# The opening of a fused attention and expert kernel: embeddings scaled earlier, the second group loaded in two parts, zeros by another engine

## The chip, the cores and the metric

The kernel runs on one core of a Trainium2 chip. The metric is the device time of one execution in microseconds (us); several executions are timed and the median is taken. A profile records one execution.

The engines are named as in the profile: PE (matrix multiply) with PEld (its weight loads), DVE (vector), ACT (scalar, activation), POOL (general) and SP (issues transfers only). Each works through its own instructions in program order and waits for others by semaphores. POOL and SP issue transfers between device memory and on-chip memory.

## The reference

Attention over 8 batches and 8 heads, with 576 positions and 64 columns, followed by a layer of eight experts of which each token takes one:

```python
cum    = cumsum(max(s, 0))
scores = q @ k.T / sqrt(64)
scores = where(causal, -1e9, scores + min(-(cum[:, None] - cum[None, :]), 0))
attn   = softmax(scores)                      # per head
x      = (attn @ v) heads side by side        # 4608 tokens x 512
en     = emb / (norm(emb) + 1e-6)             # 8 experts x 512
logits = (x / norm(x)) @ en.T / tau
e      = argmax(logits);  gate = softmax(logits)[e]
out    = gate * (max(x @ w1[e], 0) @ w2[e])
```

## The kernel before

All 64 heads are worked one after another, then the experts. Heads are numbered n and lie in groups g of four; a group's transposed queries and keys are loaded together (`load(g)`) into one of three buffers `qkbs[g % 3]`: 64 rows of Q (2560 columns, the region `0:QW`) beside 64 rows of K (2304 columns, `QW:`). Rows 64 to 127 hold ones under Q, and under K zeros with a few rows for the cumulative sums and the row maxima. `kzeros(i)` writes the zeros, `qones(i)` the ones, `krow(i)` a constant row 96 into the K side.

Products are in split precision: `qkbs` holds high parts, and `QCs`, `KCs` hold for each pair of heads a copy of the high part in one half of the rows and the low part in the other. For group 0 the high parts are made on chip (`round0`, ACT), copied (`hcopy`, ACT) and subtracted (`qlow` on DVE, `klow` on POOL). For later groups ACT writes the negated high part (`neg`) and a transfer on POOL's queue adds the original onto it (`addl`).

A head n takes these steps: `s1` to `s4` compute the scores once for the maxima of the rows (PE), `sr` and the reductions in `s3`, `s4` take them (DVE); after every second head `mrow1`, `mrow2` transpose the maxima and `sends()` sends them back into row 96 of `qkbs`. Then `ta_`, `tb_`, `tbl` compute the scores again, transposed, with the maxima and the cumulative sums inside the product; `expa`, `expb1` take the exponential on ACT; `pl_` makes the low part of the probabilities (POOL, `psub`, line 242); `pv` multiplies with V (PE). The score phase runs several heads ahead: with head n goes the score phase of head m = n + 3 in the opening.

V is not used as it is: `emm(n)` multiplies V with a matrix `en4` (PE), which holds the identity and, beside it, the scaled expert embeddings, so that attention gives the router's logits as well. `vsq` sums the squares of V (ACT), `vscale` and `vcp` scale the result. The embeddings `em` are scaled once, in these steps: `ra` (ACT: the sum of squares, its square root through logarithm and exponential), `rb` (DVE and POOL: the temperature and `en4`'s constant part), `rc` (DVE: a reciprocal), `rd` (POOL: three tiny operations that refine the root), `rc` again, `re` (POOL: `r7`, lines 567 and 568, which scale `em`), and last `r7s[0]()`, that is `r8` (PE: four transposes, line 573; DVE: two copies into `en4`).

The order on each engine is the order of the calls, written by hand (a manual schedule). `begin()` is the opening: the set-up, `rows(0)` to `rows(2)` (the score phase of the first three heads, with `heat` matmuls between, which compute nothing that is used), then a loop over n = 0, 1, 2 with the first three heads' second phase, then the part with m = 6 which starts `pv(0)`. Then the loop `step(n)` runs from n = 3. In the opening, `load(1)` brings group 1 in one transfer, and the lines around the embeddings are:

```python
        ra()
        kzeros(2)
...
            if n == 0:
                rc()
                rd()          # behind s4(m), ahead of expb1(0)
...
            if n == 1:
                sends()
                rc()
                re()          # ahead of pl_(1) on POOL
...
            if n == 1:
                addl(1, False)
                r7s[0]()
                emm(0)
```

Of the kernel before, what the change touches and what calls it, by code (L numbers as in the profile page):

```python
# [8 lines left out]
F32 = mybir.dt.float32  # L9
# [15 lines left out]
QW = HG * SP  # L25
# [81 lines left out]
def main(ctx, tc, qkh, qkc, vtin, s_in, emb, tau, w1h, w2h, out, shared, nb):  # L107
# [50 lines left out]
    nc.vector.memset(one, 1.0)  # L158

    def kzeros(i):  # L160
        nc.scalar.copy(qkbs[i][64:128, QW:], zero[64:128].to_broadcast([64, KW]))

    def round0(i):
        nc.scalar.copy(qkbs[0][0:64, 2 * SP * i:2 * SP * i + 2 * SP], qrs[i])
# [2 lines left out]
    def qones(i):  # L167
        nc.gpsimd.memset(qkbs[i][64:128, 0:QW].bitcast(F32), 1.0)

    def krow(i):  # L170
        nc.gpsimd.dma_start(qkbs[i][96:97, QW:], qkc)
    kzeros(0)
    nc.scalar.copy(qkbs[0][64:128, 0:QW], one[64:128].to_broadcast([64, QW]))
    nc.gpsimd.memset(mS, 0.0)
    nc.gpsimd.affine_select(out=mS[:, 448:576], in_=mS[:, 448:576], pattern=[[-1, 128]],
# [1 line left out]
    nc.vector.memset(tiny, 1.0e-30)  # L177
    nc.vector.memset(tri0, 0.0)
    nc.vector.memset(tri, 1.0)
    nc.vector.memset(qkbs[1][64:128, QW:].bitcast(F32), 0.0)  # L180
    nc.vector.tensor_scalar(st, st, 0.0, 8.0, op0=ALU.max, op1=ALU.mult)
    nc.vector.tensor_tensor_scan(cum, st, st, 0.0, op0=ALU.add, op1=ALU.bypass)
    nc.vector.tensor_copy(chl[:, 0, :], cum)
# [57 lines left out]
    def psub(out, a, b_):  # L241
        nc.gpsimd.tensor_tensor(out, a, b_, op=ALU.subtract)  # L242

    def load(g):
        if g >= NGg:
            return
        qkb = qkbs[g % 3]
        if g > 0:
            nc.gpsimd.dma_start(qkb[0:64, :], qkh[g], **(dict(max_dma_last_dim=4864) if g < 3 else {}))
        G[g] = dict(QB=qkb[:, 0:QW].rearrange("p (h s) -> p h s", h=HG), KB=qkb[:, QW:].rearrange("p (h s) -> p h s", h=HG))  # L250

    def loadc(g):
# [11 lines left out]
    def vsq(b, ps):  # L264
        if not 0 <= b < nb:
            return
        if ps[0] == 0:
            VB[b]["sq"] = p2.tile([128, 4], F32, name="sq")
        for p in ps:
            nc.scalar.activation(vjunk, vTs[b % 2][:, p], AF.Square, accum_out=VB[b]["sq"][:, p:p + 1])  # L270
# [40 lines left out]
    def hcopy(g, k, i):  # L311
        if 0 <= g < NGg:
            h = pair(i)
            o, t = (KCs[g % 2][64:128, h], G[g]["KB"][0:64, h]) if k else (QCs[g % 2][0:64, h], G[g]["QB"][0:64, h, 64:SP])
            nc.scalar.copy(o, t.bitcast(F32))

    def neg(g, k, i):
        if 0 <= g < NGg:
            h = pair(i)
            o, t = (KCs[g % 2][0:64, h], G[g]["KB"][0:64, h]) if k else (QCs[g % 2][64:128, h], G[g]["QB"][0:64, h, 64:SP])  # L320
            nc.scalar.activation(o, t.bitcast(F32), AF.Copy, scale=-1.0)
# [9 lines left out]
    def klow(i):  # L331
        h = pair(i)
        psub(KCs[0][0:64, h], krs[i].rearrange("p (h s) -> p h s", h=2), G[0]["KB"][0:64, h].bitcast(F32))

    def qlow(i):
        h = pair(i)
        nc.vector.tensor_sub(QCs[0][64:128, h], qrs[i].rearrange("p (h s) -> p h s", h=2)[:, :, 64:SP], G[0]["QB"][0:64, h, 64:SP].bitcast(F32))
# [54 lines left out]
    def s3(n):  # L392
        if n >= NH:
            return
        p1 = ps_s.tile([128, 512], F32, tag="s", name="s3")
        smax_mm(n, 4, p1[:, 0:288], 0, 288)
        nc.vector.tensor_reduce(MP["4", n // 2][:, n % 2:n % 2 + 1], p1[:, 0:288], AX.X, ALU.max)  # L397
# [77 lines left out]
    def tbl(n):  # L475
        tb = HD[n]["tb"]
        for f in (hh_, hl_):
            f(n, tb[:, 512:704], 3, 384, 576)
        hh_(n, tb[:, 0:64], 4, 512, 576)
        mask(tb[:, 0:192], trim[:, 0:192])  # L480
        hl_(n, tb[:, 0:64], 4, 512, 576, True)
        mask(tb[:, 512:896].rearrange("p (a b) -> p a b", b=192)[:, :, 0:128], trib.unsqueeze(1).to_broadcast([128, 2, 128]), stop=True)
# [5 lines left out]
    def expb1(n):  # L488
        nc.scalar.activation(HD[n]["P32"][:, 576:1600], HD[n]["tb"], AF.Exp, scale=0.125)  # L489
# [435 lines left out]
    def rows(m):  # L925
        s1(m)
        heat(1)
        sr(m, 3)
        s2(m)
        heat(1)  # L930
        sr(m, 2)
        sr(m, 1)
        s3(m)
        heat(2)
        s4(m)
        heat(2)
        mrow1(m)

    def sends():
        rq.popleft()()  # L940
        aslot()

    def begin():
        make_identity(nc, ident)
        masks()
        load(0)
        loadc(1)
        nc.gpsimd.dma_start(krs[1], qkh[0][:, QW + 2 * S:])
        load(1)
        krow(0)  # L950
        krow(1)
        ra, rb, rc, rd, re = rsetup()
        rb()
        hset(0)
        for i in range(2):
            round0(i)
            hcopy(0, False, i)
            hcopy(0, True, i)
        qlow(0)
        klow(0)  # L960
        klow(1)
        ra()
        kzeros(2)
        rows(0)
        rows(1)
        sends()
        qlow(1)
        for p in range(2):
            loadt(0, pair(p))
        nc.sync.dma_start(cumd.rearrange("x r s -> r x s").bitcast(F32), chl.bitcast(F32))  # L970
        rows(2)
        hset(1)
        qones(1)
        setup2()
        neg(1, True, 0)
        for n in range(3):
            m = n + 3
            ta_(n, m)
            sr(m, 3)
            expa(n)  # L980
            if n == 0:
                neg(1, False, 0)
                neg(1, True, 1)
            if n == 1:
                sends()
                rc()
                re()
                neg(1, False, 1)
                vsq(0, range(4))
            if n == 2:  # L990
                vscale(0)
                fslot()
                while tasks:
                    slot()
                vcp(0, False)
                vcp(1, False)
            s2(m)
            tb_(n)
            sr(m, 2)
            sr(m, 1)  # L1000
            if n == 2:
                vcp(0, True)
                vcp(1, True)
            s3(m)
            tbl(n)
            s4(m)
            if n == 0:
                rc()
                rd()
            expb1(n)  # L1010
            if n == 1:
                hcopy(1, True, 0)
            mrow1(m)
            if n < 2:
                pl_(n, 0, 576, "p")
                if n == 0:
                    load(2)
                pl_(n, 576, 1600, "p")
            if n == 2:
                qones(2)  # L1020
                krow(2)
            if n == 0:
                addl(1, True)
            if n == 1:
                addl(1, False)
                r7s[0]()
                emm(0)
                emm(1, om)
        m = 6
        s1(m)  # L1030
        sr(m, 3)
        sends()
        s2(m)
        pv(0, [0, 1, 2])
        sr(m, 2)
        sr(m, 1)
        s3(m)
        emm(2)
        pv(0, [3, 4])
        s4(m)  # L1040
        hcopy(1, True, 1)
        vcp(2, False)
        hcopy(1, False, 0)
        vcp(2, True)
        hcopy(1, False, 1)
        loadc(2)
        loadt(1, pair(0))
        pl_(2, 0, 576, "p")
# [399 lines left out]
```

## Time and profile before

| | us |
|---|---|
| median of 3 runs | 780.52 (780.29 to 781.52) |
| the profiled execution | 781.86 |
| its span, first to last instruction | 780.1 |
| PE busy in it | 759.8 (97%) |
| DVE, ACT, POOL busy | 523.5, 570.9, 383.5 |
| start of the loop `step(n)` on PE | 45.9 |

A row of a timeline gives the start of an instruction from the span's start, its duration, engine and line, output and input, and in brackets how long the engine had been idle and what ended that. A row of a table of stretches gives for each engine the busy time in that stretch, and the TensorE clock that was granted (1.00 is full).

### The profile page before, as it was taken

The numbers are of one execution on the slowest core, as the hardware profiler recorded it, in microseconds if no ns is written. First come the engines' busy times: TensorE is split into PE (matmuls) and PEld (weight loads), VectorE is DVE, ScalarE is ACT, GpSimd is POOL, SyncE is SP. The second block draws the span as 40 slices with busy tenths as digits, with TensorE's granted clock in tenths as the row PEclk, the third lists the DMA queues.
The fourth block names the chain that finished last, engine by engine and source line by source line (L and its number), as shares of the span: only waits on it lengthen the run. The fifth ranks groups of instructions, "written<-read, shape, count | busy, mean of one in ns | idle before, by whom it ended". The sixth has DMA issues, their size and how long they took to land. (4 is left out here: it accounts for less than half of the span.)

```text
span 780.1 us, 19394 instructions
## 1 busy us (share of the span) xinstructions
PE 759.8 (97%) x7276; PEld 569.3 (73%) x7276; DVE 523.5 (67%) x1773; ACT 570.9 (73%) x1012; POOL 383.5 (49%) x370
## 2 busy tenths in 40 slices
PE   7699999999999999999999999999999999999997
PEld 3689999999999999996567557466475574664753
DVE  8477888888888888868675656655665466556621
ACT  9688999999999999988675767837658468376410
POOL 9766798989888798785412131221221211312001
PEclk9799999999999999999999999999999999999999
DMA  7775879797979797764634765753754558645001
GB/s 157 174 170 110 178 173 212 167 216 171 213 165 218 160 218 174 194 218 158 217 94 135 172 178 163 170 186 95 208 179 99 168 166 154 194 96 141 12 15 55
DMA packets 75936, 123.79 MB, mean 159 GB/s; under 512 B 38774, under 2 KB 39178, under 8 KB 74980
## 3 DMA queue, kind: packets, MB, share of 16 engines
q0 software_dynamic: 19568, 69.68, 38.2%
q1 hardware_dynamic: 56272, 52.84, 24.7%
q8 instruction: 58, 0.95, 0.5%
q14 instruction: 38, 0.31, 0.1%
HBM read 93.99 MB, written 21.49 MB: 148 GB/s over the span
## 5 line engine op out<-in xcount | busy, mean ns | idle before, releaser
L242 POOL TENSOR_TENSOR PL<-P 128x576 f16<-128x576 f32 (+2 forms) x128 | 205.0, 1705 | 24.7 <-ACT P L486 17.1
L852 PEld LDWEIGHTS <-wt 128*128 128x128 f16 x1536 | 149.7, 98 | 59.5 <-DVE wt L840 0.5
L852 PE MATMUL h<-xH,wt 128*128 128x320 f16 (+2 forms) x1024 | 186.7, 299 | 0.0
L882 POOL DMA_INDIRECT out<-Kx,xj x39 | 40.8, 1046 | 167.3 <-DVE Kx L881 105.9
L720 POOL DMA_INDIRECT Qx<-xs,idx x40 | 42.3, 1058 | 141.0 <-ACT hp L861 84.1
L514 PE MATMUL om<-vh,P 128*128 128x73 f16 x960 | 106.9, 199 | 0.9 <-DVE xt L539 0.6
L515 PE MATMUL om<-vl,P 128*128 128x72 f16 x960 | 106.2, 196 | 0.0
L852 PE MATMUL h<-xL,wt 128*128 128x320 f16 (+1 forms) x480 | 106.1, 297 | 0.0
L516 PE MATMUL om<-vh,PL 128*128 128x73 f16 x960 | 106.0, 197 | 0.0
L352 PE MATMUL s<-qkb 96*128 96x288 f32 (+4 forms) x272 | 97.5, 372 | 3.9 <-DVE M L397 1.7
L515 PEld LDWEIGHTS <-P 128*128 128x128 bf16 x960 | 94.6, 99 | 1.4 <-issue 0.9
L876 PE MATMUL pxs<-wt,hp 128*128 128x512 f16 x351 | 94.8, 379 | 0.0
L514 PEld LDWEIGHTS <-P 128*128 128x128 bf16 x960 | 93.7, 98 | 0.7 <-DVE xt L539 0.4
L516 PEld LDWEIGHTS <-PL 128*128 128x128 f16 x960 | 93.9, 98 | 0.0
L876 PE MATMUL pxs<-wt,hq 128*128 128x512 f16 x351 | 88.8, 379 | 0.1
L360 DVE CUSTOM_DVE_ANT_0 junk<-s,mS 128x448 bf16<-128x448 f32 (+3 forms) x144 | 73.8, 520 | 6.8 <-PE s L352 4.6
L489 ACT ACTIVATE P<-tb 128x1024 f32<-128x1024 f32 x64 | 65.2, 1018 | 3.2 <-PE tb L457 2.0
L881 DVE TENSOR_SCALAR Kx<-pxs,xj,idx 128x512 f32<-128x512 f32 x39 | 31.5, 808 | 52.6 <-PE pxs L876 37.5
L861 ACT ACTIVATE hv<-h 128x640 f16<-128x640 f32 (+2 forms) x18 | 11.6, 644 | 72.8 <-PE h L852 67.1
L876 PEld LDWEIGHTS <-hp 128*128 128x128 f16 x351 | 34.3, 98 | 41.5 <-issue 0.3
L876 PEld LDWEIGHTS <-hq 128*128 128x128 f16 x351 | 34.3, 98 | 41.2
L454 PE MATMUL tb<-QC,KC 128*128 128x448 f32 (+3 forms) x256 | 64.3, 309 | 0.0
(252 smaller groups left out, 1841.2 us busy)
## 6 DMA issues: line engine op xcount, KB each, us to landing
qkb<-qkh POOLq DMA_DIRECT2D x15, 1216.0 KB, 9.1
ring<-w2h SPq DMA_DIRECT2D x44, 256.0 KB
ring<-w1h SPq DMA_DIRECT2D x36, 256.0 KB
KC<-qkh POOLq DMA_DIRECT2D x15, 576.0 KB, 8.3
QC<-qkh POOLq DMA_DIRECT2D x15, 576.0 KB, 7.6
vT<-vtin SPq DMA_DIRECT2D x24, 320.0 KB
rw<-w1h SPq DMA_DIRECT2D x15, 256.0 KB
rw<-w2h SPq DMA_DIRECT2D x12, 256.0 KB
```

Of the source, the lines that this page charges most:

```text
L242: nc.gpsimd.tensor_tensor(out, a, b_, op=ALU.subtract)
L352: nc.tensor.matmul(out, G[g]["QB"][0:96, h, 128 * i:128 * i + 128], G[g]["KB"][0:96, h, lo:hi], start=True, stop=True)
L360: nc.vector.tensor_tensor_reduce(out=jk, in0=src, in1=ms, scale=1.0, scalar=NEG, op0=ALU.add, op1=ALU.max, accum_out=MP[n // 2][:, n % 2, ...
L454: nc.tensor.matmul(out, HD[n]["KC"][:, ks:ks + 128], HD[n]["QC"][:, qlo:qhi], start=False, stop=stop)
L489: nc.scalar.activation(HD[n]["P32"][:, 576:1600], HD[n]["tb"], AF.Exp, scale=0.125)
L514: nc.tensor.matmul(out, lh, vh[:, kb], start=(kb == 0), stop=False)
L515: nc.tensor.matmul(out[:, u:u + 72], lh, vl[:, kb], start=False, stop=False)
L516: nc.tensor.matmul(out, ll, vh[:, kb], start=False, stop=(kb == j))
L720: ins = nc.gpsimd.indirect_dma_start(out=x.bitcast(I32), out_offset=None, in_=src, in_offset=bass.IndirectOffsetOnAxis(ap=X[("i", e, t)][1 ...
L852: nc.tensor.matmul(h[:, u, 0:b - a], w[:, 128 * c:128 * c + 128], x[:, c, lo + a:lo + b], start=(c == 0 and k == 0), stop=(c == 3 and k == 2))
L876: nc.tensor.matmul(y, h[:, 128 * t:128 * t + 128], w, start=(m == 0 and k == 0), stop=(m == 7 and k == 2))
L882: nc.gpsimd.indirect_dma_start(out=out, out_offset=bass.IndirectOffsetOnAxis(ap=xf[0].bitcast(U32), axis=0), in_=ys, in_offset=None, bound ...
```

## The change

It reorders the opening. `ra()` moves between the two halves of group 0's set-up on ACT; `rc`, `rd` stand behind `rows(0)`, the second `rc` and `re` behind `rows(1)`, ahead of `klow(1)` on POOL. `r7s[0]()` moves ahead of `tbl(1)`. `load` gets the columns as an argument: K of group 1 goes where the whole load went, Q behind `sends()`. `qones(1)` moves ahead of `rows(1)`. `qlow(1)` moves from ahead of `rows(2)` to the end of n = 1. `kzeros` becomes a DVE memset; that of buffer 2 moves from ahead of `rows(0)` to the part with m = 6, and `krow(2)` behind it. `vsq(0, ...)` is split into two pairs, in n = 0 and n = 1. `neg` and `addl` of group 1 change places a little, and `addl(1, True)` goes out in two halves; `load(2)` follows it.

```diff
     def kzeros(i):
-        nc.scalar.copy(qkbs[i][64:128, QW:], zero[64:128].to_broadcast([64, KW]))
+        nc.vector.memset(qkbs[i][64:128, QW:].bitcast(F32), 0.0)
...
-    def load(g):
+    def load(g, o=slice(0, QW + KW)):
...
-            nc.gpsimd.dma_start(qkb[0:64, :], qkh[g], **(dict(max_dma_last_dim=4864) if g < 3 else {}))
+            nc.gpsimd.dma_start(qkb[0:64, o], qkh[g][:, o], **(dict(max_dma_last_dim=4864) if g < 3 else {}))
...
-        load(1)
+        load(1, slice(QW, QW + KW))
...
             hcopy(0, True, i)
+            if i == 0:
+                ra()
         qlow(0)
         klow(0)
+        rows(0)
+        rc()
+        rd()
+        qones(1)
+        rows(1)
+        rc()
+        sends()
+        load(1, slice(0, QW))
+        re()
         klow(1)
-        ra()
-        kzeros(2)
-        rows(0)
-        rows(1)
-        sends()
-        qlow(1)
...
         hset(1)
-        qones(1)
         setup2()
         neg(1, True, 0)
+        neg(1, True, 1)
...
             if n == 0:
-                neg(1, False, 0)
-                neg(1, True, 1)
+                vsq(0, (0, 1))
             if n == 1:
                 sends()
-                rc()
-                re()
                 neg(1, False, 1)
-                vsq(0, range(4))
...
             s3(m)
+            if n == 1:
+                r7s[0]()
             tbl(n)
             s4(m)
+            expb1(n)
             if n == 0:
-                rc()
-                rd()
-            expb1(n)
+                neg(1, False, 0)
             if n == 1:
+                vsq(0, (2, 3))
+            if n == 2:
                 hcopy(1, True, 0)
             mrow1(m)
+            if n == 1:
+                qlow(1)
             if n < 2:
                 pl_(n, 0, 576, "p")
                 if n == 0:
-                    load(2)
+                    addl(1, True, pair(0))
                 pl_(n, 576, 1600, "p")
             if n == 2:
                 qones(2)
-                krow(2)
             if n == 0:
-                addl(1, True)
+                addl(1, True, pair(1))
+                load(2)
             if n == 1:
                 addl(1, False)
-                r7s[0]()
                 emm(0)
                 emm(1, om)
         m = 6
+        kzeros(2)
+        krow(2)
```

More of the change, by code (lines that the diff above doesn't have):

```diff
@@ L171, in krow @@
         nc.gpsimd.dma_start(qkbs[i][96:97, QW:], qkc)
-    kzeros(0)
+    nc.scalar.copy(qkbs[0][64:128, QW:], zero[64:128].to_broadcast([64, KW]))
     nc.scalar.copy(qkbs[0][64:128, 0:QW], one[64:128].to_broadcast([64, QW]))
@@ L179, in main @@
     nc.vector.memset(tri, 1.0)
-    nc.vector.memset(qkbs[1][64:128, QW:].bitcast(F32), 0.0)
+    kzeros(1)
     nc.vector.tensor_scalar(st, st, 0.0, 8.0, op0=ALU.max, op1=ALU.mult)
```

## The prediction

> **What bounds the kernel now.** I read four views: the table of stretches (busy time of each engine, granted clock), cut where the granted TensorE clock changes; then the timelines of PE, POOL and DVE alone over the opening; then the DMA issues. From 45.9 us on the kernel is a loop bound by TensorE:
>
> ```profile
> 45.90:780.00 734.10, 726.05 (x7073) 544.94 (x7072) 494.10 (x1668) 535.64 (x973) 347.70 (x311) 1.00 0.63 159
> ```
>
> The columns are the stretch, its length, busy us (instructions) of PE, PEld, DVE, ACT and POOL, the granted clock, the DMA share and GB/s. PE is busy 726 of 734 us, so the loop is not touched by this change; only the time at which it begins can move, and a shift of that start reaches the end one for one, if no other engine is behind by then. The opening is different:
>
> ```profile
> 17.69:21.10 3.41, 1.56 (x9) 1.01 (x7) 3.20 (x13) 2.97 (x3) 3.11 (x16) 1.00 0.94 266
> 21.10:24.50 3.40, 3.40 (x17) 3.32 (x17) 1.70 (x8) 3.36 (x4) 0.00 (x0) 0.51 0.55 208
> 24.50:27.90 3.40, 3.00 (x21) 2.55 (x20) 2.80 (x15) 2.99 (x5) 2.43 (x6) 0.98 0.03 9
> 27.90:31.30 3.40, 0.00 (x0) 0.00 (x0) 0.67 (x4) 3.31 (x9) 3.30 (x4) 1.00 0.96 197
> 31.30:34.70 3.40, 1.56 (x8) 1.49 (x9) 0.38 (x2) 1.40 (x2) 3.40 (x3) 0.52 1.16 197
> 34.70:38.10 3.40, 3.40 (x16) 3.27 (x15) 0.63 (x2) 0.04 (x1) 3.36 (x3) 0.50 1.08 175
> ```
>
> Two things stand here. PE does nothing from 27.9 to 31.3, while POOL works all the time; and from 21.1 to 24.5 POOL does nothing at all. Also the clock: after a stretch in which PE worked 1.56 us of 3.4 or less, the next stretch runs at half clock (21.1, 31.3, 34.7); after 3.00 it runs full. The PE timeline (start, duration, line, output and input; in brackets the idle time before and what ended it) shows the stall:
>
> ```profile
> 19.91 0.47 PE L352 MATMUL s<-qkb 96*128 96x448 f32 x1 [0.79 <-DVE M L397]
> ...
> 24.12 0.68 PE L352 MATMUL s<-qkb 96*128 96x448 f32 x1
> ...
> 27.36 0.41 PE L352 MATMUL s<-qkb 96*128 96x288 f32 x2
> 32.61 0.59 PE L573 MATMUL pe<-ident,em 8*128 8x8 f32 x4 [4.84 <-POOL em L568]
> 33.74 1.78 PE L290 MATMUL V<-en,vT 128*128 128x144 f32 x6 [0.53 <-PE pe L573]
> 35.31 1.17 PE L290 MATMUL om<-en,vT 128*128 128x144 f32 x4
> ...
> 37.34 0.68 PE L454 MATMUL ta<-QC,KC 128*128 128x320 f32 x2
> ...
> 45.92 0.28 PE L457 MATMUL ta<-trim,identb 128*128 128x256 bf16 x1
> ```
>
> The three opening stages start at 19.91 (n=0), 24.12 (n=1) and about 36.3 (n=2); the loop (step 3) starts at 45.92. Stage 1 ends at 27.77, and then PE waits 4.84 us for `em`, the scaled embeddings. POOL's own timeline says why:
>
> ```profile
> 11.54 5.36 POOL L242 TENSOR_TENSOR KC<-vh,qkb 64x1152 fp32r<-64x1152 f32 x2
> 16.96 2.23 POOL L168 MEMSET qkb<- 64x2560 f32 x1
> ...
> 25.21 0.18 POOL L581 TENSOR_TENSOR es<-es 8x1 f32<-8x1 f32 x1 [4.12 <-DVE es L578]
> ...
> 30.41 0.48 POOL L567 TENSOR_SCALAR es<-es 8x1 f32<-8x1 f32 x1
> 31.00 1.56 POOL L568 TENSOR_SCALAR em<-em,es 8x512 f32<-8x512 f32 x1
> ```
>
> `rd` (L581) waits 4.12 us for a tiny reciprocal that DVE has queued behind the rows of head 3; L567 and L568 then stand behind stage 0's subtractions and two load issues.
>
> **The change, part by part.** *Embeddings ahead.* `rd` follows `klow(0)`, whose half of the 5.36 us ends at 14.2 (11.54 + 2.7); `rd`'s three operations need about 0.8 (25.21 to 26.0 before), the memset `qones(1)` 2.23: 17.3. There the Q half of `load(1)` is issued (0.7), then L567 and L568: 30.41 to 32.56 is 2.15, so `em` is ready at about 20.2. `klow(1)` ends at 22.9 and the small memsets at about 24.8; they are needed only by head 2. PE reaches the transposes at about 28, so the wait of 4.84 goes away wholly, with 8 us to spare. What is late next: the rows of Q, and DVE.
>
> *The load split.* One issue more on POOL, 0.7 us, which lies inside its old idle time. K goes first and ACT's two `neg(1, True, ...)` find it. Q is the danger: s1(4), the first matmul of stage 1, reads it, and everything on PE queues behind. The rows:
>
> ```profile
> qkb<-qkh POOLq DMA_DIRECT2D x3, 1216.0 KB, 8.9
> ```
>
> ```profile
> 18.50:23.25 4.75, 3.61 (x17) 3.08 (x17) 3.72 (x18) 4.27 (x5) 2.30 (x16) 0.78 0.88 317
> 11.00:17.25 6.25, 4.78 (x30) 3.07 (x29) 5.41 (x22) 5.84 (x9) 6.20 (x6) 1.00 1.19 212
> ```
>
> The first row gives 8.9 us from issue to landing for both halves, the second the stretch in which SP's loads of V (issued once the first head pair's maxima are sent) move 1.5 MB, the third the stretch in which POOL's loads move at 212 GB/s. Q is 655 KB: 3.1 us at 212. Of the old load's 8.9 us, 1.24 MB at 212 explain 5.9 and the 295 KB issued ahead of it 1.4, which leaves 1.6 of latency: 17.3 + 1.6 + 3.1 = 22.0 alone. If V and Q together (2.17 MB) move at 317 GB/s from 18.5, the last byte comes at 25.3. No row shows the two queues with large loads at once; I take the middle, 23.7. PE would be there at about 21.6 (stage 0 starts two microseconds earlier, since `qlow(1)` no longer stands ahead of head 2's rows), so it stalls some 2 us. [...]
>
> *Stage 1.* That stall leaves PE with about 1.3 us of work in the stretch 21.1 to 24.5, below the 1.56 after which the clock halved. So I cost stage 1 at stage 0's length at half clock, 24.12 - 19.91 = 4.2, not its own 3.65: 23.7 + 4.2 = 27.9. The four transposes of `em` now lie in it: 0.59, 28.5.
>
> *`qlow(1)` moved* to DVE, behind the rows of head 4, and stage 2's last matmuls on `ta` (L454, 37.34 before) need it:
>
> ```profile
> 2.11 1.98 DVE L180 MEMSET qkb<- 64x2304 f32 x1 [0.54 <-issue]
> ...
> 8.34 1.35 DVE L337 TENSOR_TENSOR QC<-vT,qkb 64x1152 fp32r<-64x1152 f32 x1
> ...
> 16.04 2.09 DVE L337 TENSOR_TENSOR QC<-vT,qkb 64x1152 fp32r<-64x1152 f32 x1
> ...
> 28.37 0.23 DVE L360 CUSTOM_DVE_ANT_0 junk<-s,mS 128x64 bf16<-128x64 f32 x1
> ...
> 42.17 0.62 DVE L360 CUSTOM_DVE_ANT_0 junk<-s,mS 128x448 bf16<-128x448 f32 x1
> ```
>
> DVE ended stage 1 at 28.60, 0.83 after PE's 27.77; so now at 29.3. `qlow(1)` takes 1.35 to 2.09, the longer where POOL subtracts beside it, as it partly will here: 1.72, so L454 runs at 31.05. Meanwhile PE does the ten V matmuls: at half clock 1.78 + 1.17, which ends at 31.4 at worst, near the same time. L454 moves from 37.34 to 31.05: **-6.3 us**.
>
> *V's squares in two pairs.* Same four ACT instructions; the first pair runs in stage 0, where ACT may wait for V's load, the second behind stage 1's exponentials. Both lie beside PE's wait for Q, and `vscale` comes later: 0 (their old place hid under the `em` wait). If the first pair is a microsecond late, it stays under that stall.
>
> *Zeros by DVE.* `kzeros(2)` leaves ACT and becomes a memset of 1.98 us, directly ahead of the reduction at 42.17, which follows the last of head 5 without a gap. PE's s2(6) and the products `pv(0)` are queued behind it. Nothing hides it: **+1.98**. The row `krow(2)` now waits for it on POOL, with `pl_(2)` queued behind; POOL is by then ahead of its old times, and head 2's products come only in step 4: 0.
>
> *The clock again.* These 2 us make PE's sparse stretch before `pv(0)` about 4.4 us long, with under 1 us of work in it: below 1.56. I expect 3.4 us at half clock on dense matmuls; it costs half of that, 1.7, if PE sets the pace throughout, and 0 if the clock holds: **+0.85**, both ends kept.
>
> *The loads behind.* `load(2)` goes out at about 29.4 in place of 27.1, behind the K halves of `addl(1)`; by 212 GB/s it lands before 39, and step 3 needs it after 43. 0.
>
> Sum: -6.3 + 1.98 + 0.85 = -3.5 us. The profiled execution lasted 781.86 (span 780.14); the runs shown have the median 780.52, so the median becomes **777.0**.
>
> **The rivals.** (A) Q lands early and the clock holds: 22.0 + 3.65 + 0.59, then DVE's 0.83 and 1.35, would give 28.4, where PE with its V matmuls at full clock is ready at about 29.0: -8.3 + 1.98 = -6.3, **774.2**. For it: POOL's load rate alone. Against: V's load in the same microseconds.
>
> [...]
>
> (B) Q lands at 25.3 or a little later, with the full clock loss and the long `qlow(1)`: L454 at 33.0, so -4.3 + 1.98 + 1.7 = -0.6, **779.9**.
>
> (C) The shift is swallowed by another engine, ACT above all, which the loop's first steps fill. Then 780.5. Against it: ACT loses the 2 us of zeros and idles over much of 31 to 38 now (1.40 and 0.04 us busy in those stretches).
>
> (D) Slower: Q stays behind V's load for as long as the old whole load took, 8.9 us, or longer. 17.3 + 8.9 = 26.2 makes the sum about 0.3; each microsecond beyond costs one on PE, so from a landing at about 27.5 on it is slower by over 0.2%: **782.1**. Against it: it is half the bytes.
>
> **How the numbers follow.** Forecast 0.50; A 0.13; A2 0.14; B 0.11; C 0.06; D 0.06. The likeliest gives 777.0, its own range 775.9 to 778.7. Stretched to A's end and most of the way to B: 774.2 to 779.4. 0.2% (1.6 us) is about what a measurement of this kernel tells from no change; faster by more ends at 779.0. Forecast, A, A2 and part of B lie there: 0.82; the rest of B and C 0.12; D 0.06.
>
> **What would show it.** `em` (L568's like) done at about 20 and no PE wait for it; s1(4) waiting for a DMA into `qkb` until about 23.7; half clock in the stretch after; L454 of stage 2 right behind `qlow(1)`, near 31; a 2 us DVE memset between heads 5 and 6 with PE idle beside it; the loop's first mask matmul near 42.4 in place of 45.92. The prediction is wrong if Q lands outside 22.0 to 25.3, if DVE has slack at the memset, or if the loop's later start is not what sets the end.

## The result, and the profile after

The changed kernel is slower. Its median is 785.0 us (782.16 to 788.53, 12 runs) against 780.81 us (780.29 to 781.77, 12 runs) for the kernel before; the ratio is 1.0054 (95% interval 1.0041 to 1.0067). The forecast was 777.0. Its profiled execution lasted 785.73 us, with a span of 784.0 (before 780.1). The changed kernel was profiled in one of its twelve executions, and these spread over 6 us where those before spread over 1.5, so what follows is shown for that one.

The first view is the table of stretches of the changed kernel (columns as in the prediction). In this profile the granted clock changes at 25.66, 35.90, 42.73 and 49.56, whole multiples of 3.41 us apart, so the cuts are laid on that grid:

```profile
22.25:25.66 3.41, 0.00 (x0) 0.00 (x0) 0.00 (x0) 2.06 (x5) 3.18 (x18) 1.00 1.09 259
25.66:29.08 3.42, 2.58 (x10) 2.44 (x11) 1.14 (x4) 2.01 (x3) 3.42 (x5) 0.50 0.82 158
29.08:32.49 3.41, 3.41 (x18) 3.04 (x17) 1.39 (x7) 1.20 (x2) 1.87 (x3) 0.50 0.80 130
32.49:35.90 3.41, 3.41 (x15) 3.17 (x14) 3.28 (x5) 2.33 (x5) 2.54 (x2) 0.50 1.04 193
35.90:39.32 3.42, 2.88 (x20) 2.46 (x19) 3.11 (x14) 1.88 (x4) 2.53 (x2) 1.00 1.15 197
39.32:42.73 3.41, 0.83 (x4) 0.27 (x2) 2.69 (x8) 2.91 (x3) 0.00 (x0) 1.00 0.62 115
42.73:46.14 3.41, 1.68 (x20) 1.58 (x21) 2.61 (x8) 0.00 (x0) 2.03 (x3) 0.50 0.06 8
46.14:49.56 3.42, 3.42 (x38) 3.33 (x35) 0.46 (x1) 1.30 (x2) 1.51 (x1) 0.50 0.74 219
```

```profile
49.88:784.00 734.12, 726.01 (x7073) 545.04 (x7072) 494.20 (x1668) 534.86 (x973) 346.77 (x311) 1.00 0.63 158
```

The loop takes 734.12 us, before 734.10. So the whole loss lies ahead of it: the loop starts at 49.88 in place of 45.92, **3.96 us later**, and that reaches the end one for one, as forecast. The stall of PE did not go, it moved: in place of a stretch without work at 27.9 there is one at 22.25. Behind it stand three stretches at half clock, and two more behind the sparse one at 39.32.

The PE timeline of the changed kernel:

```profile
20.72 0.28 PE L457 MATMUL ta<-trim,identb 128*128 128x256 bf16 x1
26.50 0.71 PE L352 MATMUL s<-qkb 96*128 96x448 f32 x1 [5.50 <-issue]
...
30.32 0.59 PE L573 MATMUL pe<-ident,em 8*128 8x8 f32 x4
...
32.33 1.79 PE L290 MATMUL V<-en,vT 128*128 128x144 f32 x6
33.91 1.17 PE L290 MATMUL om<-en,vT 128*128 128x144 f32 x4
...
36.61 0.50 PE L454 MATMUL ta<-QC,KC 128*128 128x320 f32 x2 [0.52 <-DVE QC L337]
...
44.47 0.80 PE L352 MATMUL s<-qkb 96*128 96x320 f32 x2 [2.90 <-DVE M L360]
...
49.88 0.29 PE L457 MATMUL ta<-trim,identb 128*128 128x256 bf16 x1
```

The transposes of `em` (L573) run without a wait; the 4.84 us are gone. In their place stand 5.50 us ahead of s1(4) at 26.50, put down to "issue", that is, to nothing that the profile shows. Who ends them is seen from the ACT timeline (the negation of Q, L321, waits for Q's transfer and starts 0.17 ahead of s1(4)), the POOL timeline, the DMA issues (KB, us from issue to landing) and the two queues' packets from 20.0 to 20.5:

```profile
26.33 1.16 ACT L321 ACTIVATE QC<-qkb 64x1152 fp32r<-64x1152 f32 x1 [1.98 <-DMA qkb<-qkh]
```

```profile
17.05 0.72 POOL L249 DMA_DIRECT2D qkb<-qkh  x1
...
18.23 1.56 POOL L568 TENSOR_SCALAR em<-em,es 8x512 f32<-8x512 f32 x1
...
33.36 1.89 POOL L242 TENSOR_TENSOR PL<-P 128x1024 f16<-128x1024 f32 x1 [2.41 <-ACT P L489]
```

```profile
qkb<-qkh POOLq DMA_DIRECT2D x1, 640.0 KB, 9.3
```

```profile
q1 hardware_dynamic: 39, 0.17, 81.5%
q0 software_dynamic: 8, 0.02, 11.7%
```

Q is issued at 17.05 and lands 9.3 later, at 26.35. The software queue (POOL's) shows its first packets of Q between 20.0 and 20.5, three us after the issue; from 17.0 to 20.0 the trace has 111 packets of the hardware queue (SP's, with V) and none of the software queue. And DVE:

```profile
33.38 3.08 DVE L337 TENSOR_TENSOR QC<-vT,qkb 64x1152 fp32r<-64x1152 f32 x1
...
41.77 1.98 DVE L161 MEMSET qkb<- 64x2304 f32 x1 [0.54 <-issue]
43.78 0.62 DVE L360 CUSTOM_DVE_ANT_0 junk<-s,mS 128x448 bf16<-128x448 f32 x1
```

The sum, by four landmarks (the rows above and the prediction's):

| | before | after | moved by | forecast |
|---|---|---|---|---|
| s1(4) starts | 24.12 | 26.50 | +2.38 | -0.42 |
| from there to L454 of stage 2 | 13.22 | 10.11 | -3.11 | -5.87 |
| from there to the reduction behind the zeros (42.17, now 43.78) | 4.83 | 7.17 | +2.34 | +1.98 |
| from there to the loop | 3.75 | 6.10 | +2.35 | +0.85 |
| sum | | | +3.96 | -3.46 |

### The profile page after: what moved, and what is told of

Its sections match the earlier page's. It is cut to its first block, busy times and chain, and to the rows that moved or that the text cites. A ratio compares the mean times of both kernels' runs of the same rounds, so it can differ in the third digit from the quotient of the medians.

```text
span 784.0 us, 19399 instructions
## 1 busy us (share of the span) xinstructions
PE 762.7 (97%) x7276; PEld 572.0 (73%) x7276; DVE 526.6 (67%) x1774; ACT 568.0 (72%) x1011; POOL 384.3 (49%) x372
## 5 line engine op out<-in xcount | busy, mean ns | idle before, releaser
L352 PEld LDWEIGHTS s<-qkb 96*128 96x128 f32 x272 | 51.9, 194 | 18.0 <-DVE M L360 9.0
```

What stands on the lines that cost most here:

```text
L352: nc.tensor.matmul(out, G[g]["QB"][0:96, h, 128 * i:128 * i + 128], G[g]["KB"][0:96, h, lo:hi], start=True, stop=True)
```

## The experiments

"Loop" is the start of the first mask matmul of step 3, read as at 49.88 above. The runs were made on several chips, whose kernel before had medians from 780.57 to 786.32, so each ratio is to the kernel before on the same chip.

**i3: the split undone, alone.** `load(1)` whole at its old place, all else as changed.

```diff
-        load(1, slice(QW, QW + KW))
+        load(1)
...
-        load(1, slice(0, QW))
```

> The changed kernel with the load of group 1 in one transfer at its old place, which undoes the split alone; the zeros, the squares and qlow(1) stay as changed. Theory (the split is the main loss, since the late Q also costs the full clock in stage 1): first matmul of stage 1 at about 21.5, L454 of stage 2 at 31 to 32.5 (qlow(1) still 3.1 beside POOL's subtraction), loop at 43 to 45.5, time 779 to 781 on a chip like the first. Rival (the split costs only the 2.4 us by which stage 1 began late): loop at 47.5, time 782.6.

Measured: 779.29 us (778.21 to 780.24), before 780.57; ratio 0.9980 (0.9971 to 0.9990), faster than before. Its PE timeline:

```profile
21.54 0.44 PE L352 MATMUL s<-qkb 96*128 96x448 f32 x1
...
29.74 0.43 PE L454 MATMUL ta<-QC,KC 128*128 128x320 f32 x2
...
37.52 0.80 PE L352 MATMUL s<-qkb 96*128 96x320 f32 x2 [2.90 <-DVE M L360]
...
43.12 0.28 PE L457 MATMUL ta<-trim,identb 128*128 128x256 bf16 x1
```

The split of the load alone costs 49.88 - 43.12 = 6.76 us of opening between these two profiles (the two ratios differ by 0.0074, some 5.8 us); without it the change gains. L454 comes 7.60 earlier than before (29.74 against 37.34). But from L454 to the loop it takes 13.38, as in the changed kernel (13.27) and not as before (8.58): the zeros and the clock behind them cost 4.8, where the forecast had 2.83. L454 came even earlier than the 31 to 32.5 expected, since `qlow(1)` took 1.67 here and not 3.1 (below).

**e2, h3, f3: why Q is late.** e2 issues Q ahead of `qones(1)`; h3 leaves Q and sends a small store ahead of V's loads on SP; f3 sends V's loads on POOL's queue, behind Q.

```diff
# e2
+        load(1, slice(0, QW))
         qones(1)
...
-        load(1, slice(0, QW))
# h3
+        nc.sync.dma_start(cumd.rearrange("x r s -> r x s").bitcast(F32), chl.bitcast(F32))
         for p in range(2):
             loadt(0, pair(p))
-        nc.sync.dma_start(cumd.rearrange("x r s -> r x s").bitcast(F32), chl.bitcast(F32))
# f3
         load(1, slice(0, QW))
+        for p in range(2):
+            VB.setdefault(0, dict(vh=vhs[0]))
+            nc.gpsimd.dma_start(vTs[0][:, pair(p)], vtin[0, :, pair(p)])
...
-        for p in range(2):
-            loadt(0, pair(p))
```

> The changed kernel with one issue moved: the Q half of group 1 is issued ahead of the memset of ones instead of behind it, near 14.9 in place of 17.05. Theory (shared engines): Q came late because V's load, 1.3 MB on SP's queue, ran in the same microseconds from 18.5 on; issued 2.2 us earlier, most of Q is through before V starts, and it lands near 20.5, so stage 1 starts near 21 in place of 26.5 and the loop 4 to 6 us earlier: 779 to 781. Rival (a latency of 9.2 us from issue, whatever else runs): it lands at 24.1, stage 1 starts 2.3 us earlier, 782 to 783.

> The changed kernel with two lines of SP's queue exchanged: the store of the cumulative sums goes ahead of V's first loads, so V is issued 0.7 us later, behind Q's issue at 17.05. Theory (a race: whichever of Q and V reaches the transfer engines first is served first): Q's first bytes come near 18.4 in place of 20.2, Q lands at 23.5 to 24.5, stage 1 starts 2 to 3 us earlier, and the loop 1 to 3 us earlier, the rest going into stretches at half clock. Rival: the store itself takes V's place in front of Q, no change.

> The changed kernel with V's first loads moved from SP's queue to the general engine's queue, behind Q of group 1. Issue of Q stays near 17.05. Theory (Q came late since V's packets were served first and then alternately): alone it lands after 1.6 + 3.1 us, near 22, and stage 1 starts at 22 in place of 26.5; V's squares then wait, which is the price. Rival (the latency is the general engine's own, which is busy with em and head pair 1's subtraction when the transfer is issued): the first bytes still come near 20, landing 23.5 or later.

Measured: e2 784.96 us, ratio 1.0013 (0.9998 to 1.0028), loop at 44.25. h3 784.93 us, ratio 1.0050 (1.0036 to 1.0065), loop at 49.57. f3, one run, 789.91 us beside 786.32, loop at 49.35. In all three Q is early: s1(4) starts at 23.72, 23.28 and 23.38 in place of 26.50. h3 changes the order of SP's transfers alone and leaves Q's issue where it was, at 17.04: so the place behind V's first load is shown to be worth 3.2 us. Q lands 6.0 after its issue there, and its first packets move between 18.0 and 18.5, two us sooner than in the changed kernel:

```profile
q0 software_dynamic: 3, 0.01, 20.7%
```

POOL's memset ahead of Q's issue and the issue itself stand at 14.87 and 17.04, in the changed kernel at 14.88 and 17.05, and POOL's order is the same in both, so the delay is not POOL's own, as the rival of f3 had it. Yet in h3 the loop is no earlier. Its SP, ACT and PE timelines say why:

```profile
17.76 1.31 SPq L262 DMA_DIRECT2D vT<-vtin  x2
```

```profile
25.37 0.74 ACT L270 ACTIVATE vjunk<-vT 128x640 bf16<-128x640 f32 x1 [5.67 <-DMA vT<-vtin]
```

```profile
23.28 0.44 PE L352 MATMUL s<-qkb 96*128 96x448 f32 x1 [2.33 <-POOL vh L206]
...
28.02 1.01 PE L450 MATMUL tb<-qkb 128*128 128x448 f32 x2 [3.07 <-ACT P L489]
```

Now V is late. ACT's first pair of squares, which the change put into stage 0 ahead of `expb1(0)`, waits 5.67 us for V; the exponential stands behind it, and PE waits 3.07 us for that. f3 shows the same (5.71 and 3.04). Whichever of the two went first in these runs, the other was late (in the changed kernel ACT waits 1.99 us for V, at 21.75, and Q takes 9.3). In e2 the third transfer is late, the 5 KB of row maxima that stage 0 itself needs (issued between 17.0 and 18.0, when 120 packets of POOL's queue move):

```profile
21.27 0.50 PE L450 MATMUL ta<-qkb 128*128 128x256 f32 x2 [2.13 <-DMA qkb<-mr]
...
38.57 0.80 PE L352 MATMUL s<-qkb 96*128 96x320 f32 x2 [2.90 <-DVE M L360]
```

e2 thus gets 5.6 of the split's 6.76 us back (49.88 to 44.25) and still loses the zeros' wait (2.90 at 38.57). Its profiled execution took 783.72 us, 1.0 less than the median before on that chip; others of its twelve took up to 787.88, and where they lost it was not seen.

**i1, i2: is it the size of Q's packets?** In the changed kernel's trace 69 packets of Q carry 0.18 MB (20.5 to 21.0) and 40 of V 0.20 MB (19.5 to 20.0), which agrees with 2560 bytes a packet of Q, a quarter of its row of 10240, and 5120 of V. i1 makes Q's 5120, i2 1280 (24 with 0.12 MB from 19.0 to 19.5, 101 with 0.13).

```diff
-            ... (dict(max_dma_last_dim=4864) if g < 3 else {}))
+            ... (dict(max_dma_last_dim=5120 if g == 1 and o == slice(0, QW) else 4864) if g < 3 else {}))   # i2: 1280
```

> The changed kernel, and the transfer of Q is cut into packets of 5120 bytes in place of 2560 (a row of 10240 bytes in two pieces, not four); nothing else. Theory (turns by packet): from 22.5 to 24.5 the changed kernel's profile has 16 packets from each queue in each half microsecond, V's of 5.1 KB and Q's of 2.6 KB, so Q gets a third of the bytes; about 0.26 MB of Q are left at 22.0, and with packets as long as V's they need 1.6 us in place of 2.9: the first matmul of stage 1 at 25.2 (24.8 to 25.6) instead of 26.50, the loop 1.3 us earlier (48.6), time about 783.7 on a chip like the first. Rival (only the order counts: V's packets were there first): 26.3 to 26.7, loop and time as changed, 785.0.

> The same with packets of 1280 bytes (eight pieces to a row). Theory (turns by packet): about 200 packets are left when the second half of V begins at 22.0; at 16 in each half microsecond they need 6.2 us, less what V's end at about 26 gives back: the first matmul of stage 1 at 28 to 30, loop at 51 to 53. Rival (only the order counts): 26.3 to 26.7, loop 49.9.

Measured: i1 785.0 us (783.94 to 786.01), ratio 1.0063 (1.0046 to 1.0080), loop 48.10; i2, one run, 785.82 us beside 780.57, loop 49.27. Q landed after 7.1 and 6.7 us, at about 24.2 and 23.8. Neither theory holds: the smallest packets were not slowest. (From 22.5 to 24.5 the changed kernel has 16 packets of V in each half microsecond, and of Q 11, 16, 16 and 22; that the queues take turns by packet is not shown.) What size alone does is not shown, since V's issue moved as well. What differed from the changed kernel was again who came first. i1's SP timeline and PE timeline:

```profile
17.48 0.94 SPq L262 DMA_DIRECT2D vT<-vtin  x2
```

```profile
24.31 0.44 PE L352 MATMUL s<-qkb 96*128 96x448 f32 x1 [2.88 <-POOL PL L209]
```

V was issued at 17.48 here and at 18.03 in i2; in the changed kernel at 17.06, level with Q:

```profile
16.24 0.78 SPq L443 DMA_DIRECT2D qkb<-mr  x1
17.06 0.94 SPq L262 DMA_DIRECT2D vT<-vtin  x2
```

V's issue follows the row maxima on SP, and those move by up to a microsecond between the profiled executions (issued at 16.20 to 17.21), while POOL issues Q at 17.04 to 17.06 in each of them. Two profiles with V at 17.02 and 17.06 have s1(4) at 27.06 and 26.50; five with V at 17.48 to 18.03 and Q ahead of it land Q by 24.3. In these seven profiles it is a race that half a microsecond decides (17.06 against 17.48), and the size of the packets does not show beside it: f1, below, with 2560 bytes and V at 17.55, starts s1(4) at 24.27; there and in i1 a memset of POOL (L209) ends the wait, and Q was there by then. In i2 the maxima paid, as in e2:

```profile
23.75 0.51 PE L450 MATMUL ta<-qkb 128*128 128x256 f32 x2 [4.46 <-DMA qkb<-mr]
```

**e4: the embeddings alone.** The kernel before with `ra`, `rc`, `rd`, `re` and `r7s[0]()` moved as in the change, and with them `klow(1)`, which now stands behind `re` on POOL.

```diff
             hcopy(0, True, i)
+            if i == 0:
+                ra()
         qlow(0)
         klow(0)
-        klow(1)
-        ra()
         kzeros(2)
         rows(0)
+        rc()
+        rd()
         rows(1)
+        rc()
         sends()
+        re()
+        klow(1)
         qlow(1)
...
             if n == 1:
                 sends()
-                rc()
-                re()
...
             s3(m)
+            if n == 1:
+                r7s[0]()
             tbl(n)
             s4(m)
-            if n == 0:
-                rc()
-                rd()
...
                 addl(1, False)
-                r7s[0]()
```

> The kernel before with one part of the change alone: the embeddings' steps early (the sum of squares between the halves of group 0's set-up, the refinement behind the first rows, the scaling ahead of head pair 1's subtraction, the transposes in stage 1). Load, zeros, the second qlow and V's squares stay as before. Theory: the 4.84 us wait for em goes, nothing takes its place but V's squares, which stood under it (3.4 us on ScalarE ahead of stage 1's second exponential): loop near 41 to 42, 776 to 777. Rival: V's squares or the general engine take the whole of it back, and the time stays at 780 to 781.

Measured: 785.37 us (before 784.76), ratio 1.0011 (1.0002 to 1.0020); loop 45.39. The wait for `em` is gone, and at most half a microsecond comes of it at the loop (45.92 and, in h4 below, 45.49 before). Its DVE and PE timelines:

```profile
16.77 5.15 DVE L337 TENSOR_TENSOR QC<-vT,qkb 64x1152 fp32r<-64x1152 f32 x1
```

```profile
22.63 0.27 PE L457 MATMUL ta<-trim,identb 128*128 128x256 bf16 x1 [4.11 <-DVE M L360]
...
36.51 0.53 PE L450 MATMUL ta<-qkb 128*128 128x256 f32 x2 [2.97 <-DMA qkb<-mr]
```

Two things take its place. The move itself makes `qlow(1)` 5.15 us long, beside POOL's scaling and `klow(1)`; that delays the reductions and so stage 0 by 3.8 us (its mask matmul stood at about 18.85). And what the 4.84 us had covered shows up: the maxima for stage 2, of which PE now waits out 2.97. They are sent at about 29.48, an estimate: their row on DVE (L440) starts at 29.18, and in e1 the transfer follows that row's start by 0.30.

**e1, e3: the zeros in stage 0.** `kzeros(2)` at the end of n = 0; e3 also undoes the split.

```diff
+            if n == 0:
+                kzeros(2)
...
         m = 6
-        kzeros(2)
```

> The changed kernel with one call moved: the zeros of buffer 2 (1.98 us on VectorE) are written at the end of stage 0, where VectorE stands idle for 5.5 us while TensorE waits for group 1's Q. Theory: the 1.98 us were wholly on the path of head 6's rows, and the idle time they gave TensorE halved its clock for the two stretches after (42.9 to 49.4). Then both go: the loop starts 2.0 + 2.3 us earlier, near 45.6, and the time falls by about 4.3, to 780.7. Rival: VectorE had slack there or the half clock comes from elsewhere: then at most 2 us, 783 or more, and half clock still stands after 42.

> The changed kernel with the zeros at the end of stage 0 and group 1 loaded in one transfer at its old place. Theory: the two lost terms (the wait for Q with its half clock, the zeros with theirs) go, and the gain from the embeddings is left: stage 1 near 20.8, stage 2's last product on ta near 28 to 30, the loop near 37 to 40, 772 to 775. Rival: with both gone the general engine's queue (its subtractions for heads 0 to 2) or the loads for group 2 become the bound, and the loop starts no earlier than about 42: 777 or more.

Measured: e1 789.2 us, ratio 1.0038 (1.0009 to 1.0067), loop 50.60; e3 782.82 us, ratio 0.9979 (0.9966 to 0.9991), loop 45.17. In e1 the memset is hidden under PE's wait for Q (it runs at 22.20), yet the loop comes no earlier:

```profile
39.37 0.85 PE L450 MATMUL ta<-qkb 128*128 128x256 f32 x2 [3.29 <-DMA qkb<-mr]
```

Stage 2 now arrives sooner and waits 3.29 us for its maxima, 5 KB sent at 29.29, with a DMA share of 0.74, 1.11 and 1.17 in the three stretches from 28.97 to 39.21; in the changed kernel 5 KB sent at 16.24, with no packet moving until 17.50, were read at 18.30. So e1 does not show what hiding the zeros is worth: another wait took their place, and s1(4) started 0.56 later as well. In e3 there is no wait for Q to hide them, and they stop PE in stage 1, ahead of s2(4) (2.90 at 25.68).

**f1, f2: the zeros or the clock, late.** f1 puts `kzeros(2)`, `krow(2)` behind `s3(6)`, where DVE waits for PE; f2 keeps the changed order and puts 12 `heat` matmuls into the wait ahead of s2(6).

```diff
# f1
-        kzeros(2)
-        krow(2)
...
         s3(m)
+        kzeros(2)
+        krow(2)
# f2
         sends()
+        heat(12)
         s2(m)
```

> The changed kernel with the zeros of buffer 2 (and the constant row behind them) moved once more: behind head 6's s3, where VectorE waits 2.8 us for TensorE's products pv(0). Theory: the 1.98 us leave the path and, with them, the second stretch at half clock, so head 6's second rows follow head 5's without a gap and the loop starts about 4.3 us earlier than in the changed kernel, near 45.6: level with the kernel before. Moved to stage 0 they made things worse because Q's late landing and the late maxima hid the gain there, not because the zeros cost nothing. Rival: the half clock after 42 does not come from the zeros: then the loop starts 2 us earlier at most, 47.9.

> The changed kernel with twelve matmuls that compute nothing used, in the 2.9 us in which TensorE waits for the zeros and the reduction behind them: the wait stays, the clock should not fall. Theory: pv(0) and what stands beside it took 6.1 us from the reduction to the loop because of the half clock, 3.75 before; at full clock the loop starts 2.0 to 2.4 us earlier, 47.5 to 47.9. Rival: the length comes from a wait, not from the clock: the loop stays at 49.9.

Measured: f1 790.02 us, ratio 1.0054 (1.0027 to 1.0081), loop 46.35; f2 789.93 us, ratio 1.0040 (1.0021 to 1.0059), loop 47.32. Two rows of f2's PE timeline:

```profile
40.07 4.44 PE L198 MATMUL om<-PL 128*128 128x512 f16 x12
...
45.43 0.90 PE L290 MATMUL V<-en,vT 128*128 128x144 f32 x6
```

From s2(6) to the loop f2 takes 3.16 us (44.16 to 47.32), the changed kernel 5.41, the kernel before 3.07: **the half clock alone costs 2.25 us there**, against 0.85 forecast. (Not all of it arrives: the heat matmuls hold s2(6) back, which starts 3.72 behind the memset's start in place of 2.70.) In f1 the memset is off PE's path and s2(6) waits only 0.27, but the clock is halved all the same, by its table of stretches:

```profile
36.87:40.29 3.42, 2.00 (x13) 1.32 (x11) 3.24 (x14) 3.34 (x5) 0.44 (x1) 1.00 1.12 198
40.29:43.70 3.41, 3.14 (x26) 2.93 (x26) 1.75 (x8) 0.81 (x1) 0.00 (x0) 0.50 0.46 85
```

s2(6) to loop is 5.68 there, and L454 to loop 10.90 in place of 13.27. So the zeros are one way into the half clock and not the only one: PE is thin in this place with or without them (2.00 us of work in the stretch at 36.87 here, 0.83 in the changed kernel's at 39.32). Neither opening's gain over the changed kernel shows in its time. On that chip the loop's own length was 740.5 us in f1 and 742.5 in f2; in f2 one late step, from the mask matmul at 339.94 to the next, took 7.70 us in place of 4.66. Why stays open.

**h2, h4: what the kernel before pays for its wait.** h2 is the kernel before with `heat(20)` ahead of `r7s[0]()`, so that PE is warm behind the wait for `em`. h4 is the kernel before once more.

```diff
+                heat(20)
                 r7s[0]()
```

> The kernel before with twenty matmuls that compute nothing used, put into the 4.84 us in which TensorE waits for em. All waits stay; the clock should not fall. Theory (the clock): the transposes, the ten V matmuls and the first products of stage 2 ran at half clock from 31.3 to 38.1; the V matmuls alone took 2.95 us in place of about 1.55. The loop starts 1.5 to 2.2 us earlier, near 44, and the time falls by as much (0.2 to 0.3%). Rival: the waits behind take it back, no change.

> The kernel before once more, for a profile on this chip beside the others: the loop should start near 46 as on the first chip, and what this chip is slower by should lie behind the loop's start, in the steps in which weights begin to be loaded and in the experts' part, for this kernel as for the others.

Measured: h2 779.96 us, ratio 0.9988 (0.9979 to 0.9997), loop 43.92; h4, one run, 781.51 us, loop 45.49. The idle wait cost two prices, itself and half clock on what followed: warm, the six V matmuls take 0.97 where the prediction's row has 1.78. The transposes start at the same time in h2 and h4 (31.28 and 31.29), and from there to the loop h2 takes 12.64 us, h4 14.20: half clock cost 1.6 us there, and the time is shorter by 0.9 (0.2 to 1.6, by the ratio). (The first profile's 45.92 is no measure for h2: its transposes came at 32.61.)

```profile
26.56 4.49 PE L198 MATMUL om<-PL 128*128 128x512 f16 x20
...
32.23 0.97 PE L290 MATMUL V<-en,vT 128*128 128x144 f32 x6 [0.53 <-PE pe L573]
```

h4 has half clock also from 42.27 to 45.68 (h2 from 39.37), which the first profile of the kernel before has not. In the stretch ahead of it PE worked 2.09 us in h4 and 1.71 in h2; in the first profile, from 38.27 to 41.68, it worked 2.47 and the clock stayed full.

**f4, h1: what the reasons suggest together.** f4: load whole, the zeros behind `s3(6)`, `qlow(1)` on POOL behind `klow(1)`, `load(2)` ahead of `addl(1, True)`, which goes out whole, and `addl(1, False)` ahead of `pl_(1)`. h1: f4 with the first pair of squares behind `expb1(0)` and the zeros at the end of n = 1.

```diff
# f4 against the changed kernel
-        load(1, slice(QW, QW + KW))
+        load(1)
...
         klow(1)
+        psub(QCs[0][64:128, pair(1)], ...)       # qlow(1)
...
             if n == 1:
-                qlow(1)
+                addl(1, False)
...
-                    addl(1, True, pair(0))
+                    load(2)
...
-                addl(1, True, pair(1))
-                load(2)
+                addl(1, True)
             if n == 1:
-                addl(1, False)
...
-        kzeros(2)
-        krow(2)
...
         s3(m)
+        kzeros(2)
+        krow(2)
# h1 against f4
-            if n == 0:
-                vsq(0, (0, 1))
...
             if n == 1:
+                vsq(0, (0, 1))
                 vsq(0, (2, 3))
...
+                kzeros(2)                        # n == 1
...
-        kzeros(2)                                # m == 6
```

> The changed kernel with four repairs: group 1 in one transfer at its old place; the zeros under pv(0); the second qlow on the general engine behind head pair 1's subtraction, so that VectorE's two-input subtraction no longer meets it; group 2's load ahead of the additions to group 1. Theory: stage 1 starts near 21.5, no half clock, stage 2's last product on ta near 28.5, the loop near 37 to 38.5, so 7 to 8.5 us below the kernel before. Rival: head pair 1's maxima, a 5 KB transfer, lands late behind the general engine's loads (it took 7 and 10 us from issue in two kernels) and stage 2 waits for it: the loop at 41 or later, 3 to 5 us below the kernel before.

> The last version with two places mended that its profile showed: the first pair of V's squares goes behind stage 0's second exponential (TensorE waited 1.39 us for that exponential), and the zeros of buffer 2 go to the end of stage 1, where VectorE then idled 2.3 us (behind s3 of head 6 they cost step 4 another 1.1 us). Theory: the loop starts near 38, about 1 us before the last version's 38.94, and step 4 is back at 5.3; the time is 3 to 5 us below the kernel before. Step 7's wait for the maxima (2.0 us) may stay, since group 3's load goes out early too. Rival: what is won at the loop's start is lost again in the loop, at transfers: no more than 2 us below the kernel before.

Measured: f4 785.75 us (before there 786.32), ratio 0.9976 (0.9959 to 0.9994), loop 38.94. h1 **778.1 us** (776.88 to 779.25; before there 780.58), ratio 0.9962 (0.9950 to 0.9974), loop 39.39: by the ratios it beats both kernels. L454 of stage 2 runs at 27.31, and stages 1 and 2 have full clock throughout. But of the 6.5 us by which the loop begins earlier only some 2.5 arrive, and in f4, of 7.0, only 0.6 by the medians and 1.9 by the ratio (its loop lasts 743.8; no profile of the kernel before was taken on that chip). h1's PE timeline and its table of stretches (of its slowest execution, 779.25), in the step from the mask matmul at 56.19 to the next at 65.38:

```profile
58.76 0.54 PE L450 MATMUL ta<-qkb 128*128 128x256 f32 x2 [2.08 <-DMA qkb<-mr]
```

```profile
56.50:59.91 3.41, 1.33 (x9) 1.14 (x9) 2.48 (x11) 0.72 (x3) 0.00 (x0) 1.00 0.35 65
59.91:63.33 3.42, 3.42 (x18) 3.38 (x17) 0.79 (x3) 2.58 (x3) 1.32 (x2) 0.50 0.00 0
```

That step takes 9.19 us in place of 5.72: a wait for maxima again, and half clock behind it. Its loop takes 738.11 in place of 734.1, and this step is 3.5 of the 4.0. Why the maxima are late there was not tried.

## Why the prediction was wrong

**What held.** The loop is not touched. `em` is ready at 19.79 (forecast 20.2), and PE's wait for it goes wholly. s1(4) waits for Q. The zeros stop PE: the memset of 1.98 with 0.54 of idle time ahead of it, +2.34 against 1.98.

**The step that failed first: Q's landing.** The prediction bounded it by 22.0 and 25.3 and took the middle, 23.7; it came at 26.35. The step "If V and Q together (2.17 MB) move at 317 GB/s from 18.5, the last byte comes at 25.3" was not an upper end: Q's first packets moved only after 20.0, behind V's first load, and h3 shows this place to be worth 3.2 us. The row of 8.9 us from issue to landing, which the prediction had and gave to rival D because Q is "half the bytes", came nearer (9.3 measured). One of the sums in this place does not come out of its rows: D's +0.3 holds only with rival B's clock and `qlow(1)`, with the forecast's it is -1.0. The race could be seen in advance, in a row of the kernel before that the prediction did not read, its SP timeline:

```profile
16.90 0.94 SPq L262 DMA_DIRECT2D vT<-vtin  x2
```

V's loads are issued at 16.90 there, and the forecast's own time for Q was 17.3: Q second, by little. The prediction took V from the stretch at 18.5 instead, where its bytes flow, and let both share from then on. The mechanism that came was rival D's, not the forecast's. D priced that landing at +0.3, and the other 3.7 us lie in the terms that follow. Against the forecast the misses are: s1(4) +2.80, from there to the V matmuls +1.04, from there to L454 +1.72 (`qlow(1)` 1.36 of it), the zeros +0.36, the clock behind them +1.50; 7.42 in all, from -3.46 to +3.96.

**The clock in stages 1 and 2, mis-sized.** The forecast had one stretch at half clock (stage 1 at 4.2 us instead of 3.65). The stall is a stretch with 0.00 us of work, and three half stretches follow: s1(4) to the V matmuls is 5.83 us with the transposes (forecast 4.79), and the V matmuls take 1.79 and 1.17. In e2, at full clock, the same way takes 3.98, and the V matmuls 0.98 and 0.65 (27.70 and 28.52). The V matmuls' own half clock is off the path: L454 waits 0.52 for `qlow(1)`.

**`qlow(1)`, mis-sized.** Forecast 1.72, the middle of 1.35 and 2.09; measured 3.08. In these profiles the length is not a matter of a middle but of when POOL's subtraction ends. In the changed kernel POOL's subtraction runs from 33.36 for 1.89 us, and `qlow(1)` begins 0.02 later and ends 1.21 us after POOL does: as if it waited for the other to end and then took nearly its 1.35. The same pair stands in e3, f1, h3 and i1 (3.08 or 3.09). In e4 it is 5.15, which ends 1.2 us after POOL's `klow(1)`; in e2 it begins while POOL only issues transfers, and takes 1.35 (28.73); in i3 it begins 0.15 ahead of the end of POOL's and takes 1.67. In the prediction's row of before, 2.09 from 16.04 ends 1.23 after POOL's 16.90. What holds `qlow(1)` up is not shown. With the 1.23 of that row the forecast would have been POOL's end plus 1.2, once both started together.

**The clock behind the zeros, mis-sized.** 0.85 forecast, the half of the 1.7 that one stretch at half clock would cost; two half stretches came, the first again thin (1.68 us of work), and f2 isolates 2.25.

**What was costed at nothing and was not.** "If the first pair is a microsecond late, it stays under that stall": V's squares stand ahead of `expb1(0)`, and where V is late (h3, f3) PE waits 3 us for the exponential. The maxima's transfer was not in the prediction at all; it is the next late thing in e1, e2, e4, i2 and h1. `krow(2)`, the extra issue and `load(2)` cost nothing that the profile shows.

**Rivals.** A (0.13) and A2 (0.14, Q as forecast and no loss by the clock) assumed that the clock holds; the trace of before spoke against that (half clock at 21.1 and 34.7, each after 1.56 us of work) and was right. C is ruled out by the loop's unchanged length. D was given 0.06, with slower only for a landing from 27.5 on: in i1 Q lands at 24.2, and the loop still begins at 48.10, 2.2 us later than before.

## What to carry to other kernels

A long wait is cover: before counting its removal as gain, list all that ends under it (here a 5 KB transfer and V's squares) and price each with the wait gone, beside what the change puts there anew (a subtraction, Q's load and 2 us of zeros). A transfer that is moved to a busy moment has to be priced against the others that the same event releases, with their starts moved as well; where two are issued within half a microsecond, as here (V at 17.06, Q at 17.05), take the loss of that race, 3.2 us here, as an end of the range. And an idle stretch of PE cost twice here, itself and half clock on what came behind it (4.57 us of idle time and, against h2, 1.6 of half clock in h4), so that a change which only moves the idle stretch can lose, as this one did (5.50 us of idle time and three stretches at half clock).

## What the runs showed of the hardware that was not expected

- Over the opening (10 to 62 us) of all 17 profiles, a full-clock stretch of 3.41 us in which PE worked 1.71 us or less was followed by one at half clock in 23 of 23 cases, and one with more than 2.69 in none of 106. Between 1.76 and 2.69 both happen, half clock in 8 of 50 (2.69 at 22.52 in i3, halved; 1.96 at 25.78 in h1, kept). Return to full clock took one stretch (before, 21.1) to three: in the changed kernel the stretch at 29.08 is busy for all of its 3.41 us and the next is still at half. The busy time of the trace does not explain that.
- From its issue to the matmul that waited for it, a transfer of 5 KB on SP took 2.32 us in i1 (16.66 to 18.98), about 7.0 in e4 (about 29.48 to 36.51) and 10.08 in e1 (29.29 to 39.37). The DMA share was 1.20 and 1.14 in e4's two stretches from 30.21 to 37.04, and 0.74, 1.11 and 1.17 in e1's three from 28.97 to 39.21.
- Two executions of one kernel differ in this: the kernel before has a clock of 0.50 from 42.27 to 45.68 in h4, and of 1.00 from 41.68 to 45.09 in the first profile.
